# Early w1 loads split by K groups, and the first matmuls gated slice by slice, in a LayerNorm-MLP kernel

## The chip, the cores and the metric

The kernel runs on one core of one Trainium2 chip. The metric is the device time of one execution in microseconds (us). I quote the median of several runs with the lowest and highest.

## The reference

Cut to what matters:

```python
B, S, D, F = 1, 2048, 1024, 3584          # bf16
y = (x - mean(x)) / sqrt(var(x) + 1e-5)   # over D
h = gelu(y @ w1 + b1)                     # [S, F]
out = h @ w2 + b2                         # [S, D]
```

Both products contract over the partition axis, 128 elements at a time. With 512 columns per matmul that is 4 blocks of S x 28 rows of w1 x 8 slices for the first product, and as many for the second: 1792 matmuls of 512 columns.

## The kernel before

The rows of x are normalised in tiles of 128. For the first block of four tiles, the tensor engine (PE) transposes each normalised tile into PSUM, and the scalar engine (ACT) copies the result to SBUF as `yT`. While the other tiles are still being normalised, PE begins the first product for four rows of w1 (the "first wave"), one tile (128 columns) at a time. All other rows use 512 columns. The later blocks are transposed by the vector engine (DVE) long before they are needed.

```python
N_WARM_A = 47                    # dummy matmuls ahead of the first real work
N_WARM_B = 14                    # and behind the transposes of tile 0
W1_CHUNK_COLS = (256, 256, 512, 1024, 1024, 1024)
SP_FIRST_LOADS = ("x0a", "x2", "b1", "w0", "w1", "x3", "w2")
ACT_FIRST_LOADS = ("x0b", "x1")
# ... w0 and w1 are the first two chunks: rows 0-1 and rows 2-3 of the first wave, all 8 slices each

        def ln_seq(tiles):               # DVE's order
            ...
            for i in tiles:
                for h in range(2):
                    seq.append(op_stats(i, h))           # waits for half h of x tile i
                    if h == 0 and prev is not None:
                        seq.append(op_norm(prev))        # tile i-1 is normalised behind tile i's first statistics
                seq.append(op_aggr(i))
                seq.append(op_eps(i))                    # rsqrt itself runs on POOL
                prev = i
            seq.append(op_norm(prev))

        def pe_T(i):
            ...                                          # 8 PE transposes into ps_t, waiting for y{i}
            act.op(lambda e, dst=dst, src=src: e.copy(out=dst, in_=src), waits=[f"tp{i}"], sig=f"te{i}")

        for t in range(TPB):                             # first wave: 4 tiles
            for r in range(R):                           # 4 rows of w1
                ...
                pe_cell(0, r, t, t + 1, ...)             # 8 matmuls of 128 columns
                ...
                if t + 1 < TPB and r == 0:
                    pe_T(t + 1)                          # next tile's transposes behind row 0

        def mm1_rows(b, r0):
            for r in range(r0, FT):
                if r == FT - 1:                          # the last row: four cells of 128 columns
                    for t in range(TPB):
                        s_m, s_g = mm1_unit(b, r, t, t + 1)
                        hT_ready[(b, t)] = [s_g]
                    mm1_done[b] = s_m
                else:
                    mm1_unit(b, r, 0, TPB)
```

## Time and profile before

| | before |
|---|---|
| time, median (13 runs) | 401.61 us (401.37 to 402.24) |
| span of the profile | 399.9 us |
| PE busy | 396.1 us (99%) |
| first real matmul | 8.29 us |
| transposes of tiles 0 / 1 / 2 / 3 begin | 6.47 / 8.79 / 11.25 / 13.56 us |
| last eviction begins | 397.66 us |

The page gives busy times by engine, and the chain that ended last, by engine:

```profile
span 399.9 us, 4938 instructions
...
PE 396.1 (99%) x2162; PEld 194.4 (49%) x2162; DVE 140.1 (35%) x307; ACT 84.5 (21%) x130; POOL 9.5 (2%) x23
...
PE 97%; DMA 2%; SPq 1%; DVE 0%; issue 0%
```

PE is busy in 99% of the span and is 97% of the chain. That alone does not say that PE works at its best pace. The chain in order of time does. Columns: start, length, what, number of instructions.

```profile
58.81 48.35 PE ps L365 x224
107.16 48.41 PE ps L325 x248
...
349.07 48.57 PE ps L365 x308
...
397.66 0.29 DVE o_sb L375
```

A stretch of second product (L365) with 224 matmuls of 512 columns takes 48.35 us, or 0.216 us each. The stretch of first product (L325) takes 48.41 us. Its last row consists of 32 matmuls of 128 columns where 8 of 512 would do, and that is the difference of 0.06 us. The last stretch, whose final group is cut into 128-column pieces, takes 48.57 us. The 1792 full matmuls alone are 387 us, so the rest that anyone can attack is between 14 and 15 us of the measured 401.6.

The timeline of the head shows most of that rest. Columns: start, length, engine and line, operation, operands, count, and in brackets the idle time of the engine before it and what ended it. PEld is the weight load that goes with each matmul.

```profile
1.04 5.20 PE L386 MATMUL ps<-ones 128*128 128x128 bf16 x47 [1.04 <-POOL ones L232]
...
6.47 0.62 PE L303 MATMUL ps_t<-ident,x_sb 128*128 128x128 bf16 x8 [0.24 <-DVE x_sb L255]
...
7.13 1.01 ACT L309 COPY yT_sb<-ps_t 128x1024 bf16<-128x1024 bf16 x1 [4.15 <-PE ps_t L303]
...
8.29 0.61 PE L325 MATMUL ps<-yT_sb,w_sb 128*128 128x128 bf16 x8 [0.19 <-ACT b_sb L397]
...
8.79 0.62 PE L303 MATMUL ps_t<-ident,x_sb 128*128 128x128 bf16 x8
...
9.25 1.95 PE L325 MATMUL ps<-yT_sb,w_sb 128*128 128x128 bf16 x32
...
10.05 0.69 DVE L239 BATCH_NORM_STATS2 st_sb<-x_sb 128x6 f32<-128x512 bf16 x1 [0.22 <-DMA x_sb<-in_x_dram]
10.66 0.53 DVE L255 TENSOR_SCALAR x_sb<-x_sb,mv_sb,rstd_sb 128x1024 bf16<-128x1024 bf16 x1
...
11.25 0.45 PEld L303 LDWEIGHTS ps_t<-ident,x_sb 128*128 128x128 bf16 x8 [0.23 <-DVE x_sb L255]
11.25 0.62 PE L303 MATMUL ps_t<-ident,x_sb 128*128 128x128 bf16 x8
...
11.71 1.95 PE L325 MATMUL ps<-yT_sb,w_sb 128*128 128x128 bf16 x32
...
12.96 0.55 DVE L255 TENSOR_SCALAR x_sb<-x_sb,mv_sb,rstd_sb 128x1024 bf16<-128x1024 bf16 x1 [0.66 <-POOL rstd_sb L247]
...
13.56 0.62 PE L303 MATMUL ps_t<-ident,x_sb 128*128 128x128 bf16 x8
```

Read it from the bottom up. Tile 3 is transposed (L303) at 13.56, as soon as DVE has normalised it (12.96 plus 0.55). Tile 2 is transposed at 11.25, after PE's weight load sat idle for 0.23 us. Its normalisation (10.66) stood behind the first statistics of tile 3, and those waited until 10.05 for the load of tile 3's x, "x3" (the wait shown is 0.22 us). Tile 0's transposes end near 7.1, ACT needs 1.01 us for the copy, and the first real matmul starts at 8.29. (The profile names ACT's cast of b1 as what ended that wait. By the kernel's code the matmul waits for the copy, which stands just before the cast on ACT.)

### The profile page before, as it was taken

The page shows a single profiled execution, that of the slowest core. Times are in us where ns is not written, and L with a number is a line of the kernel's source. Part 1 is how long each engine was busy: PE and PEld are TensorE (multiplying, and loading weights), DVE is VectorE, ACT ScalarE, POOL GpSimd, SP SyncE. Part 2 cuts the span into 40 slices and gives each one's busy share as a digit, 9 for nine tenths or more (in the row PEclk, how much of TensorE's full clock was granted, in tenths as well). Part 3 has the DMA queues.
Part 4 walks back from the last instruction along what each step waited for, and adds up shares of the span by engine and source line. Part 5 has one row for each costly group of instructions (what it writes and reads, how often), then busy time and mean ns, then how long its engine had stood idle before and what let it go on. Part 6 is the DMA issues. An engine that isn't in the chain of part 4 may idle for free.

```text
span 399.9 us, 4938 instructions
## 1 busy us (share of the span) xinstructions
PE 396.1 (99%) x2162; PEld 194.4 (49%) x2162; DVE 140.1 (35%) x307; ACT 84.5 (21%) x130; POOL 9.5 (2%) x23
## 2 busy tenths in 40 slices
PE   8999999999999999999999999999999999999997
PEld 7844454444444445444444444544444444544446
DVE  5208999889894004989100000001100000001101
ACT  2533340000043343000023344100003334400000
POOL 1102000100001000000000000000000000000000
DMA  8999930000000000000000000000000000000001
GB/s 254 381 375 387 386 138 15 26 15 26 27 2 0 0 2 0 28 13 26 29 13 0 2 0 0 2 26 28 13 28 13 0 2 0 2 13 26 15 26 28
DMA packets 17439, 23.65 MB, mean 59 GB/s; under 512 B 1418, under 2 KB 9738, under 8 KB 17418
## 3 DMA queue, kind: packets, MB, share of 16 engines
q1 hardware_dynamic: 17130, 22.95, 16.5%
q10 hardware_dynamic: 288, 0.39, 0.3%
q8 instruction: 17, 0.28, 0.3%
q14 instruction: 4, 0.03, 0.0%
HBM read 19.14 MB, written 4.19 MB: 58 GB/s over the span
## 4 chain that ended last, share of the span: by engine, by line
PE 97%; DMA 2%; SPq 1%; DVE 0%; issue 0%
PE ps L365 48%; PE ps L325 48%; DMA x_sb<-in_x_dram 2%; SPq L175 1%; PE ps_t L303 0%; DVE st_sb L239 0%; DVE x_sb L255 0%; DVE o_sb L375 0%
## 5 line engine op out<-in xcount | busy, mean ns | idle before, releaser
L325 PE MATMUL ps<-yT_sb,w_sb 128*128 128x512 bf16 (+1 forms) x1088 | 195.0, 341 | 0.2 <-ACT b_sb L397 0.2
L365 PE MATMUL ps<-w_sb,hT_sb 128*128 128x512 bf16 (+1 forms) x980 | 194.2, 361 | 0.0
L325 PEld LDWEIGHTS ps<-yT_sb,w_sb 128*128 128x128 bf16 x1088 | 96.0, 98 | 99.3 <-issue 0.3
L365 PEld LDWEIGHTS ps<-w_sb,hT_sb 128*128 128x128 bf16 x980 | 91.1, 98 | 101.7
L334 ACT ACTIVATE hT_sb<-ps,b_sb 128x512 bf16<-128x512 f32 (+1 forms) x124 | 79.1, 646 | 255.1 <-PE ps L325 254.5
L287 DVE STREAM_TRANSPOSE yT_sb<-x_sb 32x256 bf16<-32x256 bf16 x192 | 83.7, 436 | 32.6 <-PE ps L325 29.6
L375 DVE TENSOR_TENSOR o_sb<-ps,b_sb 128x512 bf16<-128x512 f32 (+1 forms) x35 | 22.6, 645 | 199.0 <-PE ps L365 198.9
L239 DVE BATCH_NORM_STATS2 st_sb<-x_sb 128x6 f32<-128x512 bf16 x32 | 21.6, 685 | 20.8 <-DMA x_sb<-in_x_dram 20.7
L247 POOL TENSOR_TENSOR rstd_sb<-vpe_sb,nhalf 128x1 f32<-128x1 f32 x16 | 8.8, 549 | 115.2 <-DVE vpe_sb L250 115.2
L255 DVE TENSOR_SCALAR x_sb<-x_sb,mv_sb,rstd_sb 128x1024 bf16<-128x1024 bf16 x16 | 8.7, 544 | 3.3 <-POOL rstd_sb L247 2.7
L386 PE MATMUL ps<-ones 128*128 128x128 bf16 x61 | 6.2, 292 | 1.0 <-POOL ones L232 1.0
L386 PEld LDWEIGHTS ps<-ones 128*128 128x128 bf16 x61 | 5.7, 138 | 1.1 <-POOL ones L232 1.0
L309 ACT COPY yT_sb<-ps_t 128x1024 bf16<-128x1024 bf16 x4 | 4.0, 1012 | 8.1 <-PE ps_t L303 8.1
L243 DVE BATCH_NORM_AGGREGATE mv_sb<-st_sb 128x2 f32<-128x12 f32 x16 | 3.3, 209 | 1.7
L303 PE MATMUL ps_t<-ident,x_sb 128*128 128x128 bf16 x32 | 2.5, 220 | 0.3 <-DVE x_sb L255 0.2
L250 DVE TENSOR_SCALAR vpe_sb<-mv_sb 128x1 f32<-128x1 f32 x16 | 2.5, 154 | 0.6
L303 PEld LDWEIGHTS ps_t<-ident,x_sb 128*128 128x128 bf16 x32 | 1.8, 98 | 0.9 <-DVE x_sb L255 0.7
L389 ACT ACT_TABLE_LOAD x1 | 1.3, 1283 | 1.7 <-PEq L508 1.7
L233 POOL TENSOR_SCALAR_AFFINE_SELECT ident<-ones 128x128 bf16<-128x128 bf16 x1 | 0.3, 292 | 0.1
L232 POOL MEMSET ones<- 128x128 bf16 x1 | 0.2, 205 | 0.3 <-POOLq L508 0.3
L397 ACT CAST b_sb<-ps 128x28 f32<-128x28 bf16 x1 | 0.2, 188 | 0.0
L395 PE MATMUL ps<-ident,b1r_sb 28*128 28x28 bf16 x1 | 0.2, 184 | 0.0
(6 smaller groups left out, 0.6 us busy)
## 6 DMA issues: line engine op xcount, KB each, us to landing
w_sb<-in_w_dram SPq DMA_DIRECT2D x4, 1792.0 KB, 18.0
w_sb<-in_w_dram SPq DMA_DIRECT2D x2, 2048.0 KB, 15.5
out_dram<-o_sb SPq DMA_DIRECT2D x31, 128.0 KB, 1.7
x_sb<-in_x_dram SPq DMA_DIRECT2D x3, 1024.0 KB, 14.0
w_sb<-in_w_dram SPq DMA_DIRECT2D x2, 1024.0 KB, 12.8
w_sb<-in_w_dram SPq DMA_DIRECT2D x2, 512.0 KB, 5.7
x_sb<-in_x_dram SPq DMA_DIRECT2D x2, 256.0 KB, 5.3
x_sb<-in_x_dram ACTq DMA_DIRECT2D x1, 256.0 KB, 4.0
```

What stands on the lines that cost most here:

```text
L175: dma_q[0].op(lambda e, dst=dst, src=src: e.dma_start(dst, src), sig=sig, sem="d_" + sig, inc=16)
L239: return (lambda e, i=i, h=h: e.bn_stats(st_sb[:, i, 6 * h:6 * (h + 1)], x_sb[:, i, h * HC:(h + 1) * HC]), [x_ev[i][h]], f"st{i}_{h}", 0.65)
L247: pool.op(lambda e, i=i: e.tensor_tensor(out=rstd_sb[:, i:i + 1], in0=vpe_sb[:, i:i + 1], in1=nhalf[:, i:i + 1], op=ALU.pow), waits=[f"vpe ...
L255: return (lambda e, i=i: e.tensor_scalar(out=x_sb[:, i, :], in0=x_sb[:, i, :], scalar1=mv_sb[:, i, 0:1], scalar2=rstd_sb[:, i:i + 1], op0= ...
L287: res.append((lambda e, src=src, dst=dst: e.transpose(out=dst, in_=src), waits, (f"tr{i}" if lastop else None), 0.47))
L303: pe.op(lambda e, i=i, j=j: e.transpose(out=ps_t[:, 0, j * P:(j + 1) * P], in_=x_sb[:, i, j * P:(j + 1) * P], identity=ident[:, :]), waits ...
L309: act.op(lambda e, dst=dst, src=src: e.copy(out=dst, in_=src), waits=[f"tp{i}"], sig=f"te{i}")
L325: pe.op(lambda e, b=b, r=r, dt=dt, n0=n0, n1=n1, bank=bank: e.matmul(ps_1[:, bank, n0:n1], lhsT=w1_sb[:, dt, r * P:(r + 1) * P], rhs=yT_sb ...
L334: act.op(lambda e, r=r, n0=n0, n1=n1, bank=bank: e.activation(out=hT_sb[:, r, n0:n1], in_=ps_1[:, bank, n0:n1], func=ACT.Gelu_apprx_tanh, ...
L365: pe.op(lambda e, st=st, ft=ft, c0=c0, c1=c1, bank=bank: e.matmul(ps_2[:, bank, 0:c1 - c0], lhsT=hT_sb[:, ft, st * P:(st + 1) * P], rhs=w2 ...
L375: crit.append((est[sig], (lambda e, ob=ob, c0=c0, c1=c1, bank=bank: e.tensor_tensor(out=o_sb[:, ob, c0:c1], in0=ps_2[:, bank, 0:c1 - c0], ...
L386: pe.op(lambda e: e.matmul(ps_2[:, NB2 - 1, 0:P], lhsT=ones[:, :], rhs=ones[:, :], start=True, stop=True), waits=["ones"])
```

## The change

The intent is to let PE start on half of the contraction while the other half is still on its way. The copy of a tile and the early w1 loads are split into two K groups, and the matmuls of the first wave are ordered by K group. Four further edits come with it: the last row of w1 is no longer split, x1 is loaded in halves, the warm-up matmuls are gated by the progress of DVE, and one later w1 chunk is smaller. With the whole last row, the second product also waits for each row of its input at the matmul that reads it; it waited for the last row at the first matmul. The diff, cut to its core:

```diff
-N_WARM_A = 47
-N_WARM_B = 14
-W1_CHUNK_COLS = (256, 256, 512, 1024, 1024, 1024)
+K_GROUPS = 2
+WARM_A = ((26, None), (8, "st0_0"), (8, "mv0"), (6, "rstd0"))
+N_WARM_B = 8
+W1_CHUNK_COLS = (256, 256, 512, 512, 1024, 1024)
+W1_KSPLIT_CHUNKS = 2
-SP_FIRST_LOADS = ("x0a", "x2", "b1", "w0", "w1", "x3", "w2")
-ACT_FIRST_LOADS = ("x0b", "x1")
+SP_FIRST_LOADS = ("x0a", "x2", "b1", "w0", "w1", "w2", "w3", "x3", "w4")
+ACT_FIRST_LOADS = ("x0b", "x1a", "x1b")
 ...
-            act.op(lambda e, dst=dst, src=src: e.copy(out=dst, in_=src), waits=[f"tp{i}"], sig=f"te{i}")
+            for h, (j0, j1) in enumerate(KGROUPS):
+                ...
+                act.op(lambda e, dst=dst, src=src: e.copy(out=dst, in_=src), waits=[f"tp{i}"], sig=f"te{i}_{h}")
 ...                                             # in pe_cell: each matmul waits for its own slice
-            waits = list(waits) + [f"w1c{w1_chunk_of_row(r)}"] + [yT_ev[b * TPB + t] for t in range(t0, t1)]
-            for dt in range(DT):
+            for k, dt in enumerate(dts):
+                w = (waits if k == 0 else []) + [f"w1c{w1_chunk_of(r, dt)}"]
+                w += [yT_ev[b * TPB + t][dt] for t in range(t0, t1)]
 ...                                             # the first wave
         for t in range(TPB):
-            for r in range(R):
-                pe_cell(0, r, t, t + 1, ...)
-                if t + 1 < TPB and r == 0:
+            for h, (j0, j1) in enumerate(KGROUPS):
+                for r in range(R):
+                    pe_cell(0, r, t, t + 1, ..., dts=range(j0, j1))
+                if t + 1 < TPB and h == 0:
                     pe_T(t + 1)
 ...
             for r in range(r0, FT):
-                if r == FT - 1:
-                    for t in range(TPB):
-                        s_m, s_g = mm1_unit(b, r, t, t + 1)
-                ...
+                mm1_row(b, r)
```

More of the change, by code (lines that the diff above doesn't have):

```diff
@@ L105, in bass_standalone__mixer_channel_mlp__prompt_kernel @@
     R = max(1, min(R_WAVE, FT - 2, NB1 - 1))
+    nkg = max(1, min(K_GROUPS, DT))
+    KGROUPS = [(h * DT // nkg, (h + 1) * DT // nkg) for h in range(nkg)]
     assert NB1 + NB2 + 1 <= 8
@@ L109, in bass_standalone__mixer_channel_mlp__prompt_kernel @@
     c0 = 0
-    for wdt in W1_CHUNK_COLS:
+    for n, wdt in enumerate(W1_CHUNK_COLS):
         if c0 + wdt <= F:
-            w1_chunks.append((c0, c0 + wdt))
+            if n < W1_KSPLIT_CHUNKS:
+                for j0, j1 in KGROUPS:
+                    w1_chunks.append((j0, j1, c0, c0 + wdt))
+            else:
+                w1_chunks.append((0, DT, c0, c0 + wdt))
             c0 += wdt
@@ L115, in bass_standalone__mixer_channel_mlp__prompt_kernel, with w1_chunk_of @@
         c1 = min(F, c0 + 512)
-        w1_chunks.append((c0, c1))
+        w1_chunks.append((0, DT, c0, c1))
         c0 = c1
-    def w1_chunk_of_row(r):
-        for ci, (a, b) in enumerate(w1_chunks):
-            if a <= r * P < b:
+    def w1_chunk_of(r, dt):
+        for ci, (j0, j1, a, b) in enumerate(w1_chunks):
+            if a <= r * P < b and j0 <= dt < j1:
                 assert (r + 1) * P <= b
                 return ci
-        raise AssertionError(r)
+        raise AssertionError((r, dt))
     nw2c = N_W2_CHUNKS
@@ L189, in load_w1 @@
         def load_w1(ci):
-            a, b = w1_chunks[ci]
-            dma(w1_sb[:, :, a:b], w1v[:, :, a:b], f"w1c{ci}", D * (b - a) * 2)
+            j0, j1, a, b = w1_chunks[ci]
+            dma(w1_sb[:, j0:j1, a:b], w1v[:, j0:j1, a:b], f"w1c{ci}", (j1 - j0) * P * (b - a) * 2)
             w1_issued.add(ci)
@@ L198, in issue @@
         def issue(item):
-            if item in ("x0a", "x0b"):
-                h = "ab".index(item[2])
-                dma(x_sb[:, 0, h * HC:(h + 1) * HC], xf[0:P, h * HC:(h + 1) * HC], f"x0_{h}", P * HC * 2)
+            if item[0] == "x" and item[-1] in "ab":
+                i, h = int(item[1:-1]), "ab".index(item[-1])
+                dma(x_sb[:, i, h * HC:(h + 1) * HC], xf[i * P:(i + 1) * P, h * HC:(h + 1) * HC], f"x{i}_{h}",
+                    P * HC * 2)
+                x_ev[i] = (f"x{i}_0", f"x{i}_1")
             elif item == "b1":
@@ L207, in issue @@
                 load_w1(int(item[1:]))
-        x_ev[0] = ("x0_0", "x0_1")
         dma_q[0] = act
@@ L215, in bass_standalone__mixer_channel_mlp__prompt_kernel @@
             issue(item)
-        for i in range(1, TPB):
+        for i in range(TPB):
             if i not in x_ev:
                 load_x_tile(i)
+            else:
+                for h, evn in enumerate(x_ev[i]):
+                    if evn not in est:
+                        issue(f"x{i}" + "ab"[h])
         if "b1" not in est:
@@ L288, in ops_T @@
                                 waits, (f"tr{i}" if lastop else None), 0.47))
-            yT_ev[i] = f"tr{i}"
+            yT_ev[i] = [f"tr{i}"] * DT
             return res
@@ L306, in pe_T @@
             blk, t = divmod(i, TPB)
-            src = ps_t[:, 0, 0:D].rearrange("p (j s) -> p j s", j=DT)
-            dst = yT_sb[:, blk % 2, :, t * P:(t + 1) * P]
-            act.op(lambda e, dst=dst, src=src: e.copy(out=dst, in_=src), waits=[f"tp{i}"], sig=f"te{i}")
-            yT_ev[i] = f"te{i}"
-            last_te[0] = f"te{i}"
+            evs = []
+            for h, (j0, j1) in enumerate(KGROUPS):
+                src = ps_t[:, 0, j0 * P:j1 * P].rearrange("p (j s) -> p j s", j=j1 - j0)
+                dst = yT_sb[:, blk % 2, j0:j1, t * P:(t + 1) * P]
+                act.op(lambda e, dst=dst, src=src: e.copy(out=dst, in_=src), waits=[f"tp{i}"], sig=f"te{i}_{h}")
+                evs += [f"te{i}_{h}"] * (j1 - j0)
+            yT_ev[i] = evs
+            last_te[0] = evs[-1]
         unit_n = [0]
@@ L319, in new_unit, with pe_cell @@
             return u % NB1, ([unit_gelu[u - NB1]] if u >= NB1 else [])
-        def pe_cell(b, r, t0, t1, bank, waits, sig):
+        def pe_cell(b, r, t0, t1, bank, waits, sig, dts=None):
             n0, n1 = t0 * P, t1 * P
-            waits = list(waits) + [f"w1c{w1_chunk_of_row(r)}"] + [yT_ev[b * TPB + t] for t in range(t0, t1)]
-            for dt in range(DT):
+            dts = list(range(DT)) if dts is None else list(dts)
+            waits = list(waits)
+            for k, dt in enumerate(dts):
+                w = (waits if k == 0 else []) + [f"w1c{w1_chunk_of(r, dt)}"]
+                w += [yT_ev[b * TPB + t][dt] for t in range(t0, t1)]
                 pe.op(lambda e, b=b, r=r, dt=dt, n0=n0, n1=n1, bank=bank: e.matmul(
@@ L327, in pe_cell @@
                     start=(dt == 0), stop=(dt == DT - 1)),
-                    waits=waits if dt == 0 else (), sig=(sig if dt == DT - 1 else None))
-            pe_t[0] += DT * _mm_us(n1 - n0)
-            est[sig] = pe_t[0]
+                    waits=w, sig=(sig if dt == DT - 1 else None))
+            pe_t[0] += len(dts) * _mm_us(n1 - n0)
+            if dts[-1] == DT - 1:
+                est[sig] = pe_t[0]
         def act_gelu(r, t0, t1, bank, wait_ev, sig):
@@ L338, in act_gelu, with mm1_row @@
             unit_gelu.append(sig)
-        def mm1_unit(b, r, t0, t1):
+        hT_row = {}
+        def mm1_row(b, r):
             bank, uw = new_unit()
-            sig = f"m1_{b}_{r}_{t0}"
-            pe_cell(b, r, t0, t1, bank, uw, sig)
-            act_gelu(r, t0, t1, bank, sig, f"g_{b}_{r}_{t0}")
-            return sig, f"g_{b}_{r}_{t0}"
+            sig = f"m1_{b}_{r}"
+            pe_cell(b, r, 0, TPB, bank, uw, sig)
+            act_gelu(r, 0, TPB, bank, sig, f"g_{b}_{r}")
+            hT_row[(b, r)] = f"g_{b}_{r}"
+            mm1_done[b] = sig
         grp_n = [0]
         grp_oe = []
-        hT_ready = {}
         crit = []
@@ L360, in out_chunk @@
             sig = f"m2_{ti}_{c0}"
-            waits = list(hT_ready[(b, st)]) + [f"w2c{ci}" for ci in range(nw2c)]
+            waits = [f"w2c{ci}" for ci in range(nw2c)]
             if g >= NB2:
@@ L367, in out_chunk @@
                     start=(ft == 0), stop=(ft == FT - 1)),
-                    waits=waits if ft == 0 else (), sig=(sig if ft == FT - 1 else None))
+                    waits=(waits if ft == 0 else []) + [hT_row[(b, ft)]],
+                    sig=(sig if ft == FT - 1 else None))
             pe_t[0] += FT * _mm_us(c1 - c0)
@@ L382, in out_chunk, with warm @@
             store_last[(ob, region)] = sev
-        def warm(n):
+        def warm(n, gate=None):
             for _ in range(n):
                 pe.op(lambda e: e.matmul(ps_2[:, NB2 - 1, 0:P], lhsT=ones[:, :], rhs=ones[:, :],
-                                         start=True, stop=True), waits=["ones"])
+                                         start=True, stop=True), waits=["ones"] + ([gate] if gate else []))
         act.op(lambda e: e.preload_act_table(ACT.Gelu_apprx_tanh))
-        warm(N_WARM_A)
+        for n, gate in WARM_A:
+            warm(n, gate)
         for o in ln_seq(list(range(TPB))):
@@ L400, in bass_standalone__mixer_channel_mlp__prompt_kernel @@
         for t in range(TPB):
-            for r in range(R):
-                lastt = (t == TPB - 1)
-                sig = f"m1_0_{r}_0" if lastt else f"m1_0_{r}_w{t}"
-                pe_cell(0, r, t, t + 1, wave[r][0], wave[r][1] if t == 0 else [], sig)
-                if lastt:
-                    act_gelu(r, 0, TPB, wave[r][0], sig, f"g_0_{r}_0")
-                if t + 1 < TPB and r == 0:
+            lastt = (t == TPB - 1)
+            for h, (j0, j1) in enumerate(KGROUPS):
+                for r in range(R):
+                    sig = f"m1_0_{r}" if lastt else f"m1_0_{r}_w{t}"
+                    pe_cell(0, r, t, t + 1, wave[r][0], wave[r][1] if (t == 0 and h == 0) else [], sig,
+                            dts=range(j0, j1))
+                    if lastt and j1 == DT:
+                        act_gelu(r, 0, TPB, wave[r][0], sig, f"g_0_{r}")
+                        hT_row[(0, r)] = f"g_0_{r}"
+                if t + 1 < TPB and h == 0:
                     pe_T(t + 1)
@@ L412, in mm1_rows @@
             for r in range(r0, FT):
-                if r == FT - 1:
-                    for t in range(TPB):
-                        s_m, s_g = mm1_unit(b, r, t, t + 1)
-                        hT_ready[(b, t)] = [s_g]
-                    mm1_done[b] = s_m
-                else:
-                    mm1_unit(b, r, 0, TPB)
+                mm1_row(b, r)
         mm1_rows(0, R)
```

## The prediction

> **What bounds it now.** The tensor engine: the page gives PE 396.1 us of a 399.9 us span (99%); the chain of waits puts 97% on PE, 2% on an x load. From 14.18 us on it is unbroken matmul: per block 48.41 us of first product and 48.35 of second; 48.35/224 = 0.216 us per 512-column matmul, and 1792 of those (387 us) stay. After the last matmul (397.64) come 2.3 us of eviction and store. The change can reach the 14 us head and the last w1 row of each block.
>
> **The head before (timeline).** Tile 0 is transposed from 6.47 us; the ACT copy of all 1024 columns runs 7.13 to 8.14; the first real matmul starts at 8.29. Tiles 1, 2, 3 are transposed at 8.79, 11.25, 13.56, each within 0.06 us of the end of its DVE normalisation. Tile 2's is held by tile 3's statistics, which wait for x3 (10.05). The w1 loads of rows 0-1 and 2-3 land at about 7.0 and 9.3, shortly before use.
>
> **What the change does.**
> 1. Half copies, w1 halves with own semaphores. The Trainium skill, "ScalarE: Activation LUTs", What ACT_TABLE_LOAD costs, gives 186 ns + 0.833 ns per element for an ACTIVATE with immediates; the trace's 1.01 us for 1024 agrees, so a half is estimated at 0.59 us. The first real matmul moves from 8.29 to about 7.85. By the instruction order 16, not 8, real matmuls precede tile 1's transposes, so 48, not 56, stay behind tile 3's. If the transposes keep their times, the gain is 8 x 0.056 = 0.45 us.
> 2. The last w1 row becomes one 512-column unit. Per block 32 x 0.056 = 1.79 us becomes 8 x 0.216 = 1.73. Four blocks: 0.24 us. The last GELU's wait moves to the 28th matmul of a group, 5.8 us after the row, against a 0.69 us GELU: nothing lost.
> 3. x1 in halves: tile 1's statistics may start 0.15 us earlier; the rsqrt on POOL and x3's landing absorb most: 0 to 0.1 us.
> 4. Gated warm-up matmuls (48 for 47, then 8 for 14): off the path, if the clock still rises before the real matmuls.
> 5. Smaller later w1 chunks: no PE wait is on them; 0.
>
> **Prediction.** 401.61 - 0.45 - 0.24 = 400.92; I say 400.95 us, 8 in 10 between 400.4 and 401.6. Faster by over 2%: 0.01; within 2%: 0.98; slower by over 2%: 0.01.
>
> **What would show it.** Half copies of about 0.59 us; first real matmul at 7.8 to 7.9; tile 3's transposes still near 13.56; first product of a later block 48.35 us; last matmul's end about 0.7 us before 397.64.
>
> **What would make it wrong.**
> - x3 now sits behind four issues of 0.4 to 0.58 us where it sat behind two; the bytes ahead are equal, but a later x3 delays tiles 2 and 3 one for one. 0.5 us would eat step 1.
> - Rows 2-3 of the first K half come third (estimate 8.1 to 8.3, needed at 8.3). Beyond about 8.45 PE stalls, and tile 1's transposes with it.
> - The clock: 47 warm-up matmuls took 5.20 us (0.11 each), the next 14 only 0.95, so the rise fell near 6.5. The skill's "TensorE: Matmul & The Clock Gate", Part 1, describes a free-running window of about 3.4 us that must be busy; this trace agrees. If the gated warm-up's gaps postpone the rise, the wave runs at half pace and costs 1 to 2 us.

## The result, and the profile after

| | before | after |
|---|---|---|
| time, median | 401.61 us (401.37 to 402.24, 13 runs) | 400.81 us (400.55 to 400.97, 9 runs) |
| ratio | | 0.9977, 95% interval 0.9968 to 0.9987 |
| span of the profile | 399.9 us | 398.8 us |
| first real matmul | 8.29 us | 7.83 us |
| transposes of tile 3 begin | 13.56 us | 13.19 us |
| last eviction begins | 397.66 us | 396.59 us |

A ratio is the mean time of one kernel's fast runs over the mean of the other's of the same rounds, so it is not quite the ratio of the medians. The gain of 0.8 us is small but real: the two ranges do not touch.

The chain that ended last, from the page of the changed kernel:

```profile
PE ps L344 49%; PE ps L387 49%; PE ps L409 2%; PE ps_t L316 0%; DVE o_sb L398 0%; POOL ones L245 0%; PE ps L419 0%; POOLq L529 0%
```

And the same chain in order of time:

```profile
57.92 48.35 PE ps L387 x224
106.27 48.35 PE ps L344 x224
...
348.00 48.57 PE ps L387 x308
...
396.59 0.29 DVE o_sb L398
```

Every stretch of first product (L344) is now 48.35 us, like the second product. The last stretch is as it was. The timeline of the head, in the same columns as before:

```profile
1.04 5.44 PE L409 MATMUL ps<-ones 128*128 128x128 bf16 x48 [1.04 <-POOL ones L245]
...
6.28 0.79 PE L316 MATMUL ps_t<-ident,x_sb 128*128 128x128 bf16 x8
...
7.10 1.07 ACT L324 COPY yT_sb<-ps_t 128x512 bf16<-128x512 bf16 x2 [3.62 <-PE ps_t L316]
...
7.83 1.05 PE L344 MATMUL ps<-yT_sb,w_sb 128*128 128x128 bf16 x16
...
8.72 0.61 PE L316 MATMUL ps_t<-ident,x_sb 128*128 128x128 bf16 x8
...
9.17 1.95 PE L344 MATMUL ps<-yT_sb,w_sb 128*128 128x128 bf16 x32
...
9.50 0.68 DVE L252 BATCH_NORM_STATS2 st_sb<-x_sb 128x6 f32<-128x512 bf16 x1
...
10.24 0.55 DVE L268 TENSOR_SCALAR x_sb<-x_sb,mv_sb,rstd_sb 128x1024 bf16<-128x1024 bf16 x1
...
10.96 0.61 PE L316 MATMUL ps_t<-ident,x_sb 128*128 128x128 bf16 x8
...
11.40 1.95 PE L344 MATMUL ps<-yT_sb,w_sb 128*128 128x128 bf16 x32
...
12.56 0.55 DVE L268 TENSOR_SCALAR x_sb<-x_sb,mv_sb,rstd_sb 128x1024 bf16<-128x1024 bf16 x1 [0.66 <-POOL rstd_sb L260]
...
13.19 0.61 PE L316 MATMUL ps_t<-ident,x_sb 128*128 128x128 bf16 x8
```

Two half copies take 1.07 us together, where the whole one took 1.01 (the page gives 588 ns for one; the ScalarE formula quoted in the prediction gives 612). The first real matmul no longer waits for the second half. 16 matmuls now stand ahead of tile 1's transposes (L316), where 8 stood. From there on PE has no pause: the next transposes follow at 8.72, 10.96 and 13.19, the last two each 40 operations of 0.056 us after the ones before. Two more things differ that the prediction did not count on: DVE's statistics at 9.50 show no wait for x3, and PE shows no wait before tile 2.

This pair of profiles also holds an accident. Tile 0's first statistics began at 3.32 us before and at 3.14 us after, because x0 happened to land earlier. To compare profiles I therefore cut every trace into three parts: from the start to tile 0's first statistics (the landing of x0, which is scatter), from there to the first transpose of tile 3 ("lead"), and from there to the start of the last eviction ("rest").

| profile | x0 statistics begin | lead | rest | lead + rest |
|---|---|---|---|---|
| before | 3.32 | 10.24 | 384.10 | 394.34 |
| r12, before again | 3.40 | 10.02 | 384.10 | 394.12 |
| after | 3.14 | 10.05 | 383.40 | 393.45 |
| r2, w1 whole | 3.42 | 10.49 | 383.40 | 393.89 |
| r3, x1 whole | 3.60 | 10.03 | 383.41 | 393.44 |
| r4, last row split | 3.54 | 10.02 | 383.65 | 393.67 |
| r5, one group | 3.44 | 10.34 | 383.86 | 394.20 |
| r6, before with x1 halves | 3.51 | 10.48 | 384.10 | 394.58 |
| r7, ungated warm-up | 3.43 | 10.03 | 383.42 | 393.45 |
| r8, no warm-up | 3.50 | 12.75 | 383.41 | 396.16 |
| r9, one group, w1 halves | 3.43 | 10.03 | 383.86 | 393.89 |
| r10, four groups | 3.47 | 10.03 | 383.19 | 393.22 |
| r11, four groups, other tail | 3.47 | 10.03 | 383.05 | 393.08 |

All in us; lead and rest are differences of two start times of that kernel's timeline. The start of tile 0's statistics stands for the landing of its x. The experiments below are read against this table. r1 is not in it, because its transposes stand at another place.

### The profile page after: what moved, and what is told of

It is laid out like the page before. It is cut to its first block, busy times and chain, and to the rows that moved or that the text cites. A ratio compares the mean times of both kernels' runs of the same rounds, so it can differ in the third digit from the quotient of the medians.

```text
span 398.8 us, 4718 instructions
## 1 busy us (share of the span) xinstructions
PE 395.4 (99%) x2061; PEld 190.2 (48%) x2061; DVE 140.1 (35%) x307; ACT 82.3 (21%) x122; POOL 9.5 (2%) x23
## 4 chain that ended last, share of the span: by engine, by line
PE 99%; issue 0%; DVE 0%; POOL 0%; POOLq 0%
PE ps L344 49%; PE ps L387 49%; PE ps L409 2%; PE ps_t L316 0%; DVE o_sb L398 0%; POOL ones L245 0%; PE ps L419 0%; POOLq L529 0%
## 5 line engine op out<-in xcount | busy, mean ns | idle before, releaser
L344 PE MATMUL ps<-yT_sb,w_sb 128*128 128x512 bf16 (+1 forms) x992 | 194.8, 358 | 0.1
L344 PEld LDWEIGHTS ps<-yT_sb,w_sb 128*128 128x128 bf16 x992 | 91.7, 98 | 102.0 <-issue 0.2
L354 ACT ACTIVATE hT_sb<-ps,b_sb 128x512 bf16<-128x512 f32 x112 | 76.6, 687 | 257.2 <-PE ps L344 257.2
L324 ACT COPY yT_sb<-ps_t 128x512 bf16<-128x512 bf16 x8 | 4.3, 588 | 7.0 <-PE ps_t L316 7.0
L316 PE MATMUL ps_t<-ident,x_sb 128*128 128x128 bf16 x32 | 2.6, 228 | 0.0
L316 PEld LDWEIGHTS ps_t<-ident,x_sb 128*128 128x128 bf16 x32 | 2.1, 104 | 0.0
```

Source lines behind the costliest of these rows:

```text
L316: pe.op(lambda e, i=i, j=j: e.transpose(out=ps_t[:, 0, j * P:(j + 1) * P], in_=x_sb[:, i, j * P:(j + 1) * P], identity=ident[:, :]), waits ...
L344: pe.op(lambda e, b=b, r=r, dt=dt, n0=n0, n1=n1, bank=bank: e.matmul(ps_1[:, bank, n0:n1], lhsT=w1_sb[:, dt, r * P:(r + 1) * P], rhs=yT_sb ...
L354: act.op(lambda e, r=r, n0=n0, n1=n1, bank=bank: e.activation(out=hT_sb[:, r, n0:n1], in_=ps_1[:, bank, n0:n1], func=ACT.Gelu_apprx_tanh, ...
```

## The experiments

Each kernel was built from the changed one unless said otherwise. All were correct. "Before" is the kernel before, run in the same rounds on the same chip; its medians were 401.54 (r1 to r4), 401.58 (r5 to r8) and 401.64 us (r9 to r11). The changed kernel itself was timed in other rounds; as the kernel before moved by only 0.1 us between rounds, I take a difference from the changed kernel's 400.81 us as good to about 0.1 us.

**My theory:** the gain is work taken away from behind tile 3's transposes, plus the whole last row. **The rivals:** the gain came from earlier landings of x, from the warm-up, or from something in the waits of the last row.

### r1: one K group (a faulty undo)

```diff
-K_GROUPS = 2
+K_GROUPS = 1
-SP_FIRST_LOADS = ("x0a", "x2", "b1", "w0", "w1", "w2", "w3", "x3", "w4")
+SP_FIRST_LOADS = ("x0a", "x2", "b1", "w0", "w1", "x3", "w2")
```

> The changed kernel with one K group instead of two: one ACT copy of 1024 columns per tile, whole w1 loads of 256 columns in the old order; whole last row, split x1 and gated warm-up stay. Theory A (the gain of the head is the 8 matmuls that no longer stand behind tile 3's transposes): first real matmul back at about 8.3 us instead of 7.83, 56 instead of 48 matmuls after tile 3's transposes, time 0.35 to 0.45 us above the changed kernel (about 401.2 us). Rival B (the head's gain came from x3 and x0 landing earlier, whatever the groups): transposes of tile 3 stay near 13.2 us and the time stays within 0.15 us of the changed kernel. Also told apart: if x3 lands at about 10.0 us again and not at 9.4, it was the halved w1 loads that brought it forward, and tile 3's transposes go back to about 13.5.

With one group the w1 loads are whole as well, since they are split by the same constant. Measured: 405.01 us (404.81 to 405.7, 4 runs), 4.2 us above the changed kernel. Neither theory had this. PE's timeline shows why:

```profile
8.44 1.95 PE L344 MATMUL ps<-yT_sb,w_sb 128*128 128x128 bf16 x32 [0.53 <-ACT b_sb L421]
10.22 0.61 PE L316 MATMUL ps_t<-ident,x_sb 128*128 128x128 bf16 x8
11.93 1.96 PE L344 MATMUL ps<-yT_sb,w_sb 128*128 128x128 bf16 x32 [1.10 <-ACT yT_sb L324]
```

With a single group, "behind the first group" means behind all 32 matmuls of a tile. So the next tile's transposes stood directly ahead of the matmuls that need them, and PE waited 1.10 us for the copy, three times. It was my error and no fair undo, but it shows the second role of the groups: the matmuls placed behind the transposes are what hides the copy. x3 landed at 9.74 us here and at 9.79 in r3, between the two values that the expectations name, so that test decided nothing.

### r2: halves in the copies and the order, but whole w1 loads

```diff
-W1_KSPLIT_CHUNKS = 2
+W1_KSPLIT_CHUNKS = 0
-SP_FIRST_LOADS = ("x0a", "x2", "b1", "w0", "w1", "w2", "w3", "x3", "w4")
+SP_FIRST_LOADS = ("x0a", "x2", "b1", "w0", "w1", "x3", "w2")
```

> The changed kernel, two half copies and matmuls by K half kept, but each early w1 chunk loaded whole, in the old order. Theory A (halved loads are needed by the new order, since the first K half of rows 2 and 3 is wanted at 8.28 us and the whole second chunk lands only near 9.3): PE stalls about 1.0 us before the matmuls of row 2, tiles 1 to 3 are transposed about 1 us later, time 0.8 to 1.0 us above the changed kernel (401.6 to 401.8 us, no better than before). Rival B (the stall is absorbed, because the DVE chain was the limit of the head, not PE): stall seen, but tile 3's transposes still near 13.2 us and the time within 0.2 us of the changed kernel.

Measured: 401.29 us (401.04 to 401.94), 0.48 us above the changed kernel. The stall is there:

```profile
7.88 0.61 PE L344 MATMUL ps<-yT_sb,w_sb 128*128 128x128 bf16 x8
8.99 0.62 PE L344 MATMUL ps<-yT_sb,w_sb 128*128 128x128 bf16 x8 [0.50 <-DMA w_sb<-in_w_dram]
```

PE waits 0.50 us for the second chunk, which landed at about 8.94 us in this run and not at the 9.3 us of the profile before. That makes the stall shorter than I expected, and about 0.2 us of it cost nothing, because tile 3 had to wait that long for DVE anyway (see r3). The table says where the rest went: lead 10.49 instead of 10.05, rest unchanged. The halved loads do carry the new order: without them most of the gain of the order is lost. The Trainium skill, "Perfetto Trace Analysis", DMA Optimizations, says of splitting DMAs into smaller chunks that it "may allow some to start sooner". This run agrees in that the matmuls of rows 2 and 3 start sooner behind halves, worth 0.44 us of lead.

### r3: x1 in one load

```diff
-ACT_FIRST_LOADS = ("x0b", "x1a", "x1b")
+ACT_FIRST_LOADS = ("x0b", "x1")
```

> The changed kernel with x1 loaded whole by one issue as before. Theory A (PE is the limit of the head from 7.83 us on, DVE has 0.08 to 0.24 us of slack at each tile): time within 0.15 us of the changed kernel; tile 1's statistics start near 5.1 us instead of 4.86. Rival B (the split x1 started the DVE chain earlier and carried 0.2 to 0.4 us to tile 3): tile 3's transposes move from 13.19 to 13.4 or later and the time rises 0.2 us or more. x3's landing near 9.4 us means that x1's split did not bring it forward; near 10.0 us that it did.

Measured: 400.96 us (400.77 to 401.07), within 0.15 us; lead plus rest is 393.44 against 393.45. Splitting x1 is worth nothing on the path. Theory A's reason needs a correction, though. In this profile the first real matmul began 4.47 us after tile 0's statistics, and in the changed kernel's 4.69 us after, because tile 0's transposes there ran before PE had reached full pace (0.79 us for eight instead of 0.62). Yet tile 3 was transposed after nearly the same lead, 10.03 and 10.05. Two chains end there. DVE's, from x0 to tile 3, allows 10.02 to 10.03 us in every profile without a late load. PE's has 96 operations of 0.056 us, thus 5.36 us, from its first real matmul to tile 3's transposes: 4.47 + 5.36 = 9.83 here, so DVE sets tile 3 with 0.2 us to spare for PE, and 4.69 + 5.36 = 10.05 in the changed kernel's profile, where PE does (tile 3 was normalised 0.08 us before). The two are level there, so an earlier start of PE gains nothing more.

### r4: the last row split again

```diff
             for r in range(r0, FT):
-                mm1_row(b, r)
+                if r == FT - 1:
+                    for t in range(TPB):
+                        bank, uw = new_unit()
+                        sig = f"m1_{b}_{r}_{t}"
+                        pe_cell(b, r, t, t + 1, bank, uw, sig)
+                        act_gelu(r, t, t + 1, bank, sig, f"g_{b}_{r}_{t}")
+                    hT_row[(b, r)] = f"g_{b}_{r}_{TPB - 1}"
+                    mm1_done[b] = sig
+                else:
+                    mm1_row(b, r)
```

> The changed kernel with the last row of w1 in every block done as four cells of 128 columns again. Theory A: the chain shows 48.41 us of first product per block instead of 48.35, in all 4 x 0.06 = 0.24 us, time about 401.05 us. Rival B (the split costs more than its matmuls, through its waits for banks and GELUs, or the whole row costs a wait at the second product): a difference of 0.5 us or more, or none, and idle time of PE at the border of the two products.

Measured: 401.25 us (400.97 to 402.06). The rest grew from 383.40 to 383.65, thus 0.25 us, with lead 10.02. That is theory A's 0.24 us. The median moved by more, 0.44 us, against runs of the changed kernel taken at another time; x0 came late in the profiled run (3.54) and two of the five runs were above 401.7, so I take the trace's figure for the size. No wait of PE for the GELUs shows in either version.

### r5: the mended undo: one group, transposes behind row 0 as before

```diff
 (as r1, and)
-                if t + 1 < TPB and h == 0:
-                    pe_T(t + 1)
+                    if t + 1 < TPB and r == 0:
+                        pe_T(t + 1)
```

> Mends the first run, where the single group also put the transposes of the next tile right ahead of that tile's matmuls, so that PE sat through transposes' drain and the 1.01 us copy three times (1.10 us each). Here: one K group, whole w1 loads and old load order, but the next tile's transposes stand after row 0's 8 matmuls as in the kernel before, so 24 matmuls cover the copy. Theory A: no 1.10 us waits any more, the first real matmul about 0.45 us later than with half copies (from the end of tile 0's transposes: about 1.2 us instead of 0.75), 56 matmuls behind tile 3's transposes, time 0.45 us above the changed kernel, 401.25 to 401.3 us. Rival B (the head's gain came from earlier landings): time within 0.15 us of the changed kernel, 400.8 to 400.95 us.

Measured: 401.40 us (401.10 to 401.71), 0.59 us above the changed kernel. The rest is 383.86, that is 0.46 us more: eight more matmuls of 128 columns behind tile 3's transposes, 8 x 0.056 = 0.45. Rival B falls. The lead is 10.34, that is 0.3 us longer, and DVE and PE say why:

```profile
10.26 0.69 DVE L252 BATCH_NORM_STATS2 st_sb<-x_sb 128x6 f32<-128x512 bf16 x1 [0.38 <-DMA x_sb<-in_x_dram]
...
11.46 0.45 PEld L316 LDWEIGHTS ps_t<-ident,x_sb 128*128 128x128 bf16 x8 [0.39 <-DVE x_sb L268]
```

x3 came late again (0.38 us of wait), now in a kernel with split x1. Among the loads, all that it shares with the kernel before and not with the changed one is the two whole w1 loads ahead of x3.

### r6: the kernel before, with x1 in halves

```diff
-ACT_FIRST_LOADS = ("x0b", "x1")
+ACT_FIRST_LOADS = ("x0b", "x1a", "x1b")
```

> The kernel before with x1 loaded in two halves and nothing else. In the traces so far x3 landed at 10.0 us with x1 and w1 whole, at 9.7 with either one split, at 9.4 with both split, and DVE wants it at 9.8. Theory C (the part of the gain that the prediction left out is x3's landing): x3 lands near 9.7, DVE no longer waits for it, tiles 2 and 3 are transposed about 0.2 us earlier relative to tile 1, time about 401.4 us against 401.55 to 401.6. Rival (x1's split does nothing for the path): wait for x3 at about 10.0 us stays, same time as before within 0.1 us.

Measured: 402.13 us (401.52 to 402.95) against 401.58; ratio 1.0013, interval 0.9999 to 1.0027, so the interval holds 1: the same, and at any rate not faster. Theory C falls as I put it:

```profile
10.48 0.69 DVE L241 BATCH_NORM_STATS2 st_sb<-x_sb 128x6 f32<-128x512 bf16 x1 [0.53 <-DMA x_sb<-in_x_dram]
...
11.68 0.62 PE L305 MATMUL ps_t<-ident,x_sb 128*128 128x128 bf16 x8 [0.35 <-DVE x_sb L257]
```

x3 was later than ever (10.48), PE waited 0.35 us for tile 2, and the lead is 10.48. I had read an effect of the x1 halves out of single profiles, where there was scatter.

### r7: the old warm-up

```diff
-WARM_A = ((26, None), (8, "st0_0"), (8, "mv0"), (6, "rstd0"))
-N_WARM_B = 8
+WARM_A = ((47, None),)
+N_WARM_B = 14
```

> The changed kernel with the old warm-up: 47 matmuls with no gates, 14 after tile 0's transposes. Theory A (the gates are off the path): the 47 end near 6.2 us, before tile 0 is normalised (6.2 to 6.6 us); the 14 take 0.95 us at full clock and end near 8.1 us, about 0.3 us after the first half copy, so the first real matmul starts at about 8.1 instead of 7.83 and the time rises 0.2 to 0.3 us. Rival B (the gates delay the clock's rise and cost time): time falls below the changed kernel by 0.1 us or more, tile 0's transposes take 0.62 us in every profile.

Measured: 400.89 us (400.79 to 401.5); lead plus rest 393.45, exactly the changed kernel's. The first real matmul started at 7.97 us, 4.54 us after tile 0's statistics, 0.07 us later than in r3, and it made no difference, because DVE set tile 3 (4.54 + 5.36 = 9.90, below DVE's 10.03). Theory A's sign for the start was right and its cost of 0.2 to 0.3 us was wrong. The gates neither help nor harm.

### r8: no warm-up

```diff
-WARM_A = ((26, None), (8, "st0_0"), (8, "mv0"), (6, "rstd0"))
-N_WARM_B = 8
+WARM_A = ()
+N_WARM_B = 0
```

> The changed kernel with no warm-up matmuls at all. Theory A (the array starts at half pace and rises only after a busy stretch): 128-column matmuls of the first wave come every 0.107 us instead of 0.056[...], and the time rises by 1 to 3 us, with more spread between runs than the changed kernel's 0.4 us. Rival B (the warm-up has no effect on this head, since DVE paces it): within 0.2 us.

Measured: 402.90 us (402.75 to 403.61, 4 runs), 2.1 us above the changed kernel. The profile is of the slowest of the four runs (403.61 us); in it the lead is 2.7 us longer (12.75) and the rest unchanged (383.41), so all of the loss is in the lead. In PE's timeline:

```profile
8.38 1.87 PE L344 MATMUL ps<-yT_sb,w_sb 128*128 128x128 bf16 x16 [0.63 <-ACT yT_sb L324]
...
10.90 3.29 PE L344 MATMUL ps<-yT_sb,w_sb 128*128 128x128 bf16 x32
...
14.47 1.95 PE L344 MATMUL ps<-yT_sb,w_sb 128*128 128x128 bf16 x32
```

The 32 matmuls from 10.90 on take 3.29 us, and the 16 ahead of them took 1.87, while 32 take 1.95 us from 14.47 on. So the warm-up earns about 2 us, and the risk that I named in the prediction was a real one that did not come true. The mean granted clock reads 1.0 in this run as in all others and does not show this slow start: the clock records in r8's packed trace begin only at 13.69 us, where the start-to-start distance falls from 0.107 to 0.056 us, and the mean counts the time before them as full.

### r9: one group with halved w1 loads

```diff
 (the changed kernel, with r5's place of the transposes, and)
-K_GROUPS = 2
+K_GROUPS = 1
+LOAD_GROUPS = 2        # w1 loads still in two halves by K
```

> The mended one-group run (one copy of 1024 columns, transposes behind row 0) but with the early w1 loads in halves, so it differs from the changed kernel only in copies and matmul order, and from the mended run only in the w1 loads. Theory D (halved w1 loads bring x3 in at 9.4 to 9.75 us, whole ones at 9.7 to 10.5, and DVE wants it at 9.6 to 9.85): no wait of DVE for x3, no wait of PE before tile 2's transposes, time about 0.45 us above the changed kernel (401.25 to 401.3 us) and 0.1 to 0.2 us below the mended one-group run's 401.40, with less spread. Rival: x3 lands near 10 us here too and the time equals the mended run's; then the halves had nothing to do with it.

Measured: 401.36 us (401.19 to 401.39). No wait for x3, none of PE before tile 2; lead 10.03, rest 383.86:

```profile
3.43 1.29 DVE L254 BATCH_NORM_STATS2 st_sb<-x_sb 128x6 f32<-128x512 bf16 x2 [3.43 <-DMA x_sb<-in_x_dram]
...
13.46 0.62 PE L318 MATMUL ps_t<-ident,x_sb 128*128 128x128 bf16 x8
...
397.32 0.29 DVE L400 TENSOR_TENSOR o_sb<-ps,b_sb 128x128 bf16<-128x128 f32 x1 [1.27 <-PE ps L389]
```

In the trace it is 0.31 us better than r5, all of it in the lead. In the medians it is only 0.04 us better, so theory D's 0.1 to 0.2 us did not show in the time, though the spread shrank from 0.61 to 0.20 us. r9 against the changed kernel leaves the copies and the order alone: rest 383.86 against 383.40, the predicted 0.45 us once more (in the medians, 0.55).

### r10: four groups

```diff
-K_GROUPS = 2
+K_GROUPS = 4
+LOAD_GROUPS = 2
 ...                                             # as r9: w1 loads in two halves
-SP_FIRST_LOADS = ("x0a", "x2", "b1", "w0", "w1", "w2", "w3", "x3", "w4")
+SP_FIRST_LOADS = ("x0a", "x2", "b1", "w0", "w2", "w1", "w3", "x3", "w4")
-                if t + 1 < TPB and h == 0:
-                    pe_T(t + 1)
+                    if t + 1 < TPB and h == 2 and r == 1:
+                        pe_T(t + 1)
```

> Goes further: four K groups of two slices, four copies of 256 columns per tile, early w1 loads still in halves but both first halves first, the next tile's transposes after 20 of the 32 matmuls of a tile. Estimate from the traced copies (1.01 us for 1024 columns, 0.59 for 512): a copy of 256 columns takes 0.38 us. Theory A (the first copy's end sets PE's start, and everything after it is PE's own work): first real matmul 0.5 us after the end of tile 0's transposes instead of 0.75, 44 matmuls behind tile 3's transposes, time 0.15 to 0.25 us below the changed kernel, 400.6 us. Rival E (DVE, with only 0.08 us to spare at tile 3 in the changed kernel's trace, is the next limit, or the quarter copy after the transposes comes too late for PE): waits of PE before the transposes or after them, and a time within 0.1 us of the changed kernel.

Measured: 400.71 us (400.28 to 400.72).

```profile
7.88 1.28 PE L346 MATMUL ps<-yT_sb,w_sb 128*128 128x128 bf16 x20
9.00 0.61 PE L318 MATMUL ps_t<-ident,x_sb 128*128 128x128 bf16 x8
...
13.50 0.62 PE L318 MATMUL ps_t<-ident,x_sb 128*128 128x128 bf16 x8
```

20 matmuls ahead of tile 1's transposes, 44 behind tile 3's. The rest is 383.19, 0.21 us less than the changed kernel's 383.40, for four matmuls fewer (4 x 0.056 = 0.22), and the lead is the usual 10.03. Both expectations are half right: the gain in the trace is theory A's, and DVE does set the lead, as rival E says. It cost nothing, because the work behind tile 3 was cut while the lead stayed. In the medians the gain is 0.10 us, less than expected and hardly beyond the spread.

### r11: four groups and another tail

```diff
 (as r10, and)
-TAIL_PIECES = 4                # last output group: 4 x 128 columns
+TAIL_CUTS = (0, 384, 512)      # 384 and 128 columns
```

> The previous run, with the last output group cut into 384 and 128 columns instead of four times 128. The chain shows the last second-product stretch at 48.57 us against 48.35 elsewhere: 112 matmuls of 128 columns against 28 of 512 columns cost 0.22 us. With 28 of 384 and 28 of 128 columns the estimate is 28 x (0.1625 + 0.0558) = 6.11 us instead of 6.25: 0.14 us off, and the last eviction and store (0.29 us and about 1.5 us) unchanged. Theory: 0.1 to 0.15 us below the previous run, about 400.45 us. Rival: the eviction and store of the 384-column piece get in the way of the last one and nothing is won.

Measured: 400.54 us (400.35 to 400.59); ratio to before 0.9972 (0.9960 to 0.9985). The rest is 383.05, 0.14 us below r10, as estimated. This is the fastest version: 1.1 us below the kernel before in the same rounds, and in the trace 0.37 us below the changed kernel (lead plus rest). It was not timed in the same rounds as the changed kernel; the medians differ by 0.27 us.

### r12: the kernel before, a second profile

No edit.

> The kernel before, unchanged, for a second profile of it. With whole w1 loads x3 has so far landed 6.2 to 6.9 us after tile 0's x, with halved ones 5.9 to 6.2 us; DVE wants it 6.4 us after. If that is so, x3 lands here 6.2 to 7.0 us after tile 0's x; from the start of tile 0's statistics to the last eviction 394.1 us (no wait for x3) to 394.7 us (a wait of 0.6), against 394.34 us in the first profile. A value below 394.0 would mean that the wait for x3 is not what the rest of the gain came from.

```profile
9.88 0.69 DVE L239 BATCH_NORM_STATS2 st_sb<-x_sb 128x6 f32<-128x512 bf16 x1
...
11.11 0.62 PE L303 MATMUL ps_t<-ident,x_sb 128*128 128x128 bf16 x8
```

Here x3 landed just in time: no wait is listed, PE goes to tile 2 without one, and lead plus rest is 394.12, against 394.34 in the first profile. The 0.22 us between the two profiles of one and the same kernel is the wait for x3.

## Why the prediction was right

The prediction said 400.95 us; the time is 400.81, well inside its range. Point by point:

1. **Half copies, eight matmuls moved (0.45 us predicted).** Right. In "rest", the changed kernel is 0.70 us below the kernel before; r4 gives 0.25 of it back and r9 0.46. The half copy took 588 ns (predicted 0.59), and the first real matmul began at 7.83 (predicted 7.8 to 7.9). The reason needs one amendment. An early start is only the means: r3, r7 and the changed kernel start at different times after x0, and are equally long. What counts is how many matmuls are left behind tile 3's transposes, and those come 10.02 to 10.05 us after tile 0's statistics in every profile in which no load is late and the warm-up stands.
2. **The last row (0.24 us predicted).** Right: each first-product stretch is 48.35 us instead of 48.41, and r4 shows 0.25.
3. **x1 in halves (0 to 0.1 us).** Right, 0 (r3).
4. **Gated warm-up (0).** Right (r7). That the warm-up itself matters was right too (r8: 2.1 us).
5. **Smaller later chunks (0).** No PE wait on a w1 load appears in the changed kernel's trace. The edit was not tried alone.

The third w1 half, which I feared would be late (estimate 8.1 to 8.3 us), landed at about 7.9 us, and PE did not stall.

Two signs that I gave were wrong. "Tile 3's transposes still near 13.56" was off by 0.37 us: 0.18 of it is the earlier x0 of that run, and about 0.2 is x3. And I listed x3 as a risk, later by its two additional issues ahead, when it came earlier. With whole w1 loads DVE lost time to x3 in three of six profiles by the listed waits (0.22, 0.38 and 0.53 us in before, r5 and r6; none listed in r1, r2 and r12). With halved loads it did so in none of eight. x3 lands 6.2 to 7.0 us after tile 0's x behind whole loads and 5.9 to 6.3 us behind halves, and DVE asks for it about 6.4 us after. This is worth 0 to 0.5 us per execution and helps to explain why the measured 0.8 us is a little more than the traced 0.70. That a risk I named turned into a small gain is luck. The landings show x3 earlier behind halves on the whole, by 0.4 us in the mean (6.12 against 6.55), but the ranges overlap, and the difference is not the same in all rounds: 6.20 and 6.21 (r1, r2) against 6.19 and 5.95 (r3, r4) in one, 6.80 and 6.95 (r5, r6) against 6.10 and 6.20 (r7, r8) in another. Why the halves bring it in earlier is not shown: the bytes ahead of x3 are the same.

What is left is clear from the table. The lead of 10 us is DVE's chain over four tiles, and the rest is 383 us of unbroken matmul. r10 and r11 took another 0.4 us out of the rest. In the lead one wait stands untouched: before tile 3's normalisation DVE sits idle for 0.66 us until POOL has done the rsqrt, in every profile. No run tried to shorten it, so what it is worth is open.

## What to carry to other kernels

When the engine that sets the time has to wait at the start for a chain on another engine, look for the last point at which that chain holds it up, and count the work left behind that point: moving work ahead of it pays, an earlier start by itself does not once the other chain is the later one. When cutting an operand into groups, cut its loads and its waits alike, and leave enough work behind each transpose to hide its copy; one group in the wrong place cost 4 us where the right cut gained 0.5. For differences of tenths of a microsecond, compare distances between instructions within a trace, so that the scatter of the first load drops out.

## What the Trainium skill lacked or had wrong

- "TensorE: Matmul & The Clock Gate", Back-to-back issue gap, gives about 81 ns and 131 ns per matmul of 128 and 512 columns as the sustained pace of a real stream of weight loads and matmuls, and calls 56 and 216 ns the isolated figures. In this stream, with a weight load for each matmul, 224 matmuls of 512 columns took 48.35 us, or 216 ns each, and 32 of 128 columns 1.79 us, or 56 ns each. The figures called isolated are the sustained ones here.
- The same page, Part 1, puts the rise of the clock at around 4 us into sustained activity, give or take 500 ns. In before, r7 and r12 all 47 warm-up matmuls, without a pause between them, came every 0.107 us, and the last began 4.9 us after the first (in r6, with the same warm-up, the rise came 4.4 us after the first). In r8 PE worked without a pause from 8.38 us on, and the distance fell from 0.107 to 0.056 us only at about 13.7 us, 5.3 us later. The free-running window that the page describes allows it; the 500 ns do not.
- The same Part 1 warns that clock events in a trace have been seen to be unreliable; it does not say that the mean granted clock of a profile can leave the slow start out altogether. It read 1.0 in r8, where the pace doubled during the first wave. Five of the 14 packed traces (before, r3, r7, r9, r12) hold no clock event at all; where PE worked through the rise without a pause (after, r8), the event, at 6.64 and 13.69 us, lies within one matmul of the change of pace.
- "DMA: Bandwidth & Descriptors" has nothing on how the size of the loads ahead on a queue changes the landing of the next one: with the same bytes ahead, x3 landed 6.2 to 7.0 us after tile 0's x behind two loads of 512 KB (six profiles), and 5.9 to 6.3 us behind four of 256 KB (eight profiles). The cause is open.
